# First channel product of the mixer: Strassen's seven block products in place of eight, with narrowed weights kept in DRAM for the second pair of batches

## The chip, the cores and the metric

The kernel runs on one core of one Trainium2 chip. The metric is the time of one execution on the device, in microseconds (us). Before the change it was 598.85 us in the median of three runs (597.46 to 599.61).

## What is computed

Decay attention for 4 batches, 8 heads, 768 positions and 64 dimensions, then a mixer on its output, both in float32:

```python
# attention, in 12 blocks of 64 positions, with a state kv_state carried along
out[:, :, sl] = ((qb @ kb^T) * Dmask) @ vb + (qb * lam_pow) @ kv_state
# mixer: x has 4 x 768 x 512; w_tok1 768 x 256, w_tok2 256 x 768, w_ch1 512 x 1536, w_ch2 1536 x 512
xt = x.transpose(0, 2, 1)
h = np.maximum(xt @ w_tok1, 0.0) @ w_tok2
u = x + h.transpose(0, 2, 1)
h2 = np.maximum(u @ w_ch1, 0.0) @ w_ch2
return (u + h2).astype(np.float32)
```

The mixer's weights arrive as float64. The part that the change touches is `u @ w_ch1`, 512 channels to 1536 hidden ones, for 4 x 768 positions.

## The kernel before

**Stages.** For each of 16 pairs of heads (`i` in the loop, with steps of later pairs mixed in) the kernel loads q, k and v, makes scores, state and outputs, and writes the result transposed into `uT[b]`: 128 partitions, 4 tiles of channels, 768 positions. `turn_back` turns it again into the high and low parts `xhi` and `xlo` that the token product takes. The token product (`token_hidden`, L450, and `token_out`, L470) is cut into 48 groups, which stand between the steps of the attention; the last ten of them (two hidden groups of 18 matmuls and eight output groups of 6, all of batch 3) are left for the first channel blocks. Then comes the channel part, over two thirds of the time.

**Precision.** Every product takes three matmuls in the type float32r: each operand is split in a high part (a rounded copy, by ScalarE) and a low part (the rest), and high x high, low x high and high x low are summed in PSUM. `split_block` does this for a block of `uT` (copy on ScalarE, L534; subtraction on GpSimd, L535).

**Channel part.** The 1536 hidden channels are cut into 6 groups of 256 (`NG`, with `JG` = 2 tiles of 128), the positions into 8 blocks of 384 (`blocks`: batch and half). The outer loop runs over groups, the inner over blocks. `mm1` sums 12 matmuls of 128x128 by 384 for one tile of hidden channels, ScalarE takes relu into `hh` (L649), VectorE the rest into `hl` (L650). `mm2` of the block before sums 6 matmuls for one tile of output channels, and VectorE adds them to `uT` (L671). So a group and a block have 24 matmuls of `mm1` and 24 of `mm2`.

**Weights.** For the next group `load_group` fetches four pieces of float64 words, and `narrow` turns each into float32: one step on ScalarE (L379), five on VectorE (L380, L383, L386, L389, L392), then a copy on ScalarE (L374) and a subtraction on GpSimd (L375). This is done once for a group, spread over the first blocks.

**What sets the order.** Each engine works through its instructions in the order in which the program writes them. Steps that are not tied to a matmul stand in a list `waiting` and are taken from it by `later(n)`, or are called between the products. PSUM has eight banks: four for the tag `sc`, one for `xT`, three for `sh`.

Of the kernel before, what the change touches and what calls it, by code (L numbers as in the profile page):

```python
# [21 lines left out]
def kernel(  # L22
# [23 lines left out]
    nc = tc.nc  # L46
# [74 lines left out]
    def load_kq(i):  # L121
        b, p = pairs[i]
        kn = ap.tile([P, NC, 2, D], F32, tag="kn", bufs=2, name=f"kn{i}")
        qn = ap.tile([P, S], F32, tag="qn", bufs=2, name=f"qn{i}")
# [18 lines left out]
    def load_v(i):  # L143
        b, p = pairs[i]
        vns[i] = vn = ap.tile([P, 2, NC, D], F32, tag="vn", bufs=3, name=f"vn{i}")
# [56 lines left out]
    def turn_k(i, g):  # L202
        kn, _ = loaded[i]
        if g == 0:
            kTs[i] = ap.tile([P, S], F32, tag="kT", bufs=2, name=f"kT{i}")
# [9 lines left out]
    def turn_q(i):  # L215
        qTs[i] = ap.tile([P, S], F32, tag="qT", bufs=2, name=f"qT{i}")
        if i >= NQ:
            nc.vector.transpose(out=qTs[i], in_=loaded[i][1])
        if i >= NKD:
            kTs[i] = ap.tile([P, S], F32, tag="kT", bufs=2, name=f"kT{i}")  # L220
# [61 lines left out]
    def scores(i):  # L282
        b, p = pairs[i]
        for g in range(2):
            sc = [bank("sc", f"sc{i}{g}{h}", 3 * P) for h in range(2)]
# [77 lines left out]
    def narrow(raw, a, sg, hi, lo, view):  # L363

# [3 lines left out]

        def split():
            nc.scalar.copy(out=hi, in_=view(af))  # L374
            nc.gpsimd.tensor_sub(out=lo, in0=view(af), in1=hi.bitcast(F32))  # L375

        waiting.extend(
            [
                lambda: nc.scalar.activation(af, high.bitcast(F32), AF.Abs),  # L379
                lambda: nc.vector.tensor_scalar(  # L380
                    out=sg, in0=high, scalar1=0x80000000, scalar2=None, op0=ALU.bitwise_and
                ),
                lambda: nc.vector.scalar_tensor_tensor(  # L383
                    out=sg, in0=low, scalar=29, in1=sg, op0=ALU.logical_shift_right, op1=ALU.bitwise_or
                ),
                lambda: nc.vector.tensor_scalar(  # L386
# [169 lines left out]
    for i in range(-2, NI):  # L556
# [57 lines left out]
        if 5 <= i < 9:  # L614
            load(i - 5)
# [157 lines left out]
```

## Time and profile before

| | us |
|---|---|
| median of 3 runs (lowest, highest) | 598.85 (597.46, 599.61) |
| span of the profiled execution, first to last instruction | 596.2 |
| TensorE matmul busy in it | 577.9 |
| VectorE busy | 349.7 |
| ScalarE busy | 155.2 |
| GpSimd busy | 138.7 |
| attention and most of the token product, up to the first channel matmul | 174.9 |
| from there to the end | 421.3 |

The page of the profile gives a span and no time of its own for the profiled execution; the median is 2.65 us above the span. Engines are PE (TensorE matmul), PEld (its weight loads), DVE (VectorE), ACT (ScalarE), POOL (GpSimd) and SP (the queue that issues most transfers). A row of the costliest groups has the line, engine, operation, output and inputs, shape and count, then busy time, the mean time of one, and the idle time of the engine before it with what ended it. A row of the chain of waits has a start, a duration and the work. A row of the timeline has the same with shapes. A row of a table by stretches has for each engine its busy time and, in brackets, how many instructions started. Matmul records overlap (each shows some 336 ns, and they start 173 to 176 ns apart), so the busy time of PE says little by itself.

### The profile page before, as it was taken

Reading aid. Unit: us, or ns where it says so; the run is one execution under the profiler, and the core shown is the slowest. Engines: PE = TensorE matmul, PEld = TensorE weight load, DVE = VectorE, ACT = ScalarE, POOL = GpSimd, SP = SyncE. Lnnn points to the kernel's source line nnn. Section 1 sums busy time; section 2 is a strip of 40 time slices with the busy share of each in tenths; the row PEclk is TensorE's granted clock in tenths of the full one; section 3 lists DMA queues with packets and bytes.
Section 4 is the critical chain, followed back from the end, with each engine's and each line's share of the span. In section 5 each row is a group of like instructions: output and inputs, shape, how many; then the busy total and the mean of one; then the engine's idle time right before and its main releaser. Section 6 shows DMA issues by size and latency. Waiting matters only on the chain.

```text
span 596.2 us, 10673 instructions
## 1 busy us (share of the span) xinstructions
PE 577.9 (97%) x4378; PEld 563.0 (94%) x4378; DVE 349.7 (59%) x663; ACT 155.2 (26%) x322; POOL 138.7 (23%) x131
## 2 busy tenths in 40 slices
PE   5988899999999999999999999999999999999997
PEld 4878798889999999999999999999999999999996
DVE  4797887886633666356533654356533664356664
ACT  3554434343232244112210221112210221101011
POOL 5665532462304367101100010001100010000000
PEclk9999999999999999999999999999999999999999
DMA  9998999999110111012100210012100200016667
GB/s 187 255 227 163 176 167 183 195 155 140 37 37 0 37 50 57 1 36 70 37 1 0 71 50 23 0 36 71 36 1 1 70 1 1 0 24 94 90 89 130
DMA packets 169680, 44.73 MB, mean 75 GB/s; under 512 B 162848, under 2 KB 164000, under 8 KB 169632
## 3 DMA queue, kind: packets, MB, share of 16 engines
q1 hardware_dynamic: 165488, 42.88, 37.4%
q10 hardware_dynamic: 4144, 1.18, 0.9%
q8 instruction: 34, 0.56, 0.4%
q14 instruction: 14, 0.11, 0.1%
HBM read 37.75 MB, written 6.29 MB: 74 GB/s over the span
## 4 chain that ended last, share of the span: by engine, by line
PE 88%; DMA 4%; DVE 4%; ACT 2%; issue 1%; SPq 0%; POOL 0%; DVEq 0%; ACTq 0%
PE ph L645 34%; PE po L666 34%; PE ph L450 6%; DMA kn<-in_k_dram 4%; PE pu L470 4%; PE xT L314 3%; PE sc L290 3%; PE xT L324 2%; PE xp L346 1%; PE kv L257 1%; DVE xlo L355 1%; DVE uT L389 1%; PE kt L208 1%; ACT qT L229 0%; PE qt L228 0%
## 5 line engine op out<-in xcount | busy, mean ns | idle before, releaser
L650 DVE SCALAR_TENSOR_TENSOR hl<-ph,hh 128x384 fp32r<-128x384 f32 x96 | 53.5, 558 | 164.9 <-ACT hh L649 164.9
L666 PE MATMUL po<-hh,c2h 128*128 128x384 f32 x384 | 129.4, 337 | 0.0
L645 PE MATMUL ph<-uh,c1h 128*128 128x384 f32 x384 | 129.2, 337 | 0.0
L645 PE MATMUL ph<-ul,c1h 128*128 128x384 f32 x384 | 129.2, 336 | 0.0
L645 PE MATMUL ph<-uh,c1l 128*128 128x384 f32 x384 | 129.1, 336 | 0.0
L666 PE MATMUL po<-hh,c2l 128*128 128x384 f32 x384 | 128.8, 335 | 0.0
L666 PE MATMUL po<-hl,c2h 128*128 128x384 f32 x384 | 128.6, 335 | 0.0
L649 ACT ACTIVATE hh<-ph 128x384 fp32r<-128x384 f32 x96 | 47.2, 492 | 299.6 <-PE ph L645 297.9
L671 DVE TENSOR_TENSOR uT<-po,uT 128x384 f32<-128x384 f32 x192 | 104.7, 552 | 23.5 <-PE po L666 23.4
L666 PEld LDWEIGHTS po<-hh,c2l 128*128 128x128 f32 x384 | 72.1, 188 | 0.0
L645 PEld LDWEIGHTS ph<-ul,c1h 128*128 128x128 f32 x384 | 72.1, 188 | 0.0
L666 PEld LDWEIGHTS po<-hl,c2h 128*128 128x128 f32 x384 | 72.1, 188 | 0.0
L645 PEld LDWEIGHTS ph<-uh,c1h 128*128 128x128 f32 x384 | 72.1, 188 | 0.0
L645 PEld LDWEIGHTS ph<-uh,c1l 128*128 128x128 f32 x384 | 72.1, 188 | 0.0
L666 PEld LDWEIGHTS po<-hh,c2h 128*128 128x128 f32 x384 | 72.0, 188 | 0.0
L375 POOL TENSOR_TENSOR c1l<-wa,c1h 128x512 fp32r<-128x512 f32 x10 | 12.9, 1290 | 179.9 <-ACT c1h L374 179.9
L535 POOL TENSOR_TENSOR ul<-uT,uh 128x384 fp32r<-128x384 f32 x32 | 36.0, 1154 | 37.5 <-ACT uh L534 37.5
L314 PE MATMUL xT<-a,vn 128*64 128x128 f32 x384 | 36.4, 280 | 1.9 <-ACT uT L331 1.9
L278 POOL COPY stb<-sv 64x320 f32<-64x320 f32 x32 | 26.4, 826 | 43.5 <-DVE sv L265 42.6
L299 DVE TENSOR_TENSOR a<-sc,mask 128x384 f32<-128x384 f32 x64 | 31.2, 550 | 5.7 <-PE sc L290 5.6
L324 PE MATMUL xT<-qs,stb 128*64 128x128 f32 x320 | 31.3, 273 | 0.0
L331 ACT COPY uT<-xT 128x384 f32<-128x384 f32 x32 | 15.3, 478 | 54.4 <-PE xT L324 54.4
(80 smaller groups left out, 758.1 us busy)
## 6 DMA issues: line engine op xcount, KB each, us to landing
raw<-in_moe_w_ch_dram SPq DMA_DIRECT2D x20, 512.0 KB, 3.6
vn<-in_v_dram SPq DMA_DIRECT2D x16, 384.0 KB, 5.5
kn<-in_k_dram SPq DMA_DIRECT2D x30, 192.0 KB, 5.3
out_dram<-y SPq DMA_DIRECT2D x108, 48.0 KB, 1.9
qn<-in_q_dram SPq DMA_DIRECT2D x44, 96.0 KB, 4.2
kr<-in_k_dram SPq DMA_DIRECT2D x32, 96.0 KB, 4.0
uT<-in_moe_w_ch_dram SPq DMA_DIRECT2D x4, 512.0 KB, 4.6
qn<-in_q_dram SPq DMA_DIRECT2D x8, 192.0 KB, 4.4
```

Of the source, the lines that this page charges most:

```text
L278: nc.gpsimd.tensor_copy(out=st[r, :, h, :], in_=sv[r].rearrange("p (e c) -> p c e", c=NC - 1))
L299: nc.vector.tensor_mul(out=a, in0=sc[h].rearrange("p (c i) -> p c i", i=P), in1=mask[:, 2 * p + h, None, :].broadcast_to([P, 3, P]),)
L314: nc.tensor.matmul(out=xT[h * D : (h + 1) * D, cs], lhsT=vns[i][:, h, c, :], rhs=weights_of[i, g, h][:, cg, :], start=(cg == 0), stop=False,)
L324: nc.tensor.matmul(out=xT[h * D : (h + 1) * D, cs], lhsT=st[:, c - 1, h, :], rhs=qss[i][:, c - 1, :], start=False, stop=(cg == 2),)
L450: nc.tensor.matmul(out=ph, lhsT=w[:, c, fs], rhs=x[:, c], start=(i == 0), stop=(i == 3 * NC - 1))
L470: nc.tensor.matmul(out=pu, lhsT=h[:, kk, cs], rhs=w[:, kk, ss], start=(i == 0), stop=(i == 3 * NK - 1))
L535: nc.gpsimd.tensor_sub(out=ul[:, t], in0=ub[:, t], in1=uh[:, t].bitcast(F32))
L645: nc.tensor.matmul(out=ph, lhsT=w[:, ct, js], rhs=x[:, ct], start=(i == 0), stop=(i == 11))
L649: nc.scalar.activation(hh, ph, AF.Relu)
L650: nc.vector.scalar_tensor_tensor(out=hl, in0=ph, scalar=0.0, in1=hh.bitcast(F32), op0=ALU.max, op1=ALU.subtract)
L666: nc.tensor.matmul(out=po, lhsT=w[:, jj, cs], rhs=h, start=(i == 0), stop=(i == 3 * JG - 1))
L671: nc.vector.tensor_add(out=ub, in0=po, in1=ub)
```

## The change

For each group of hidden channels the product of 2x2 blocks of channels by 2x2 blocks of (channel, position half) is made by Strassen's scheme in Winograd's form. A unit is now a group and a whole batch: seven products of 6 matmuls (`m1` to `m7`, 42 in all) take the place of eight (48). The sums around them are made on VectorE: of the weights once for a group (`split_c1`: four sums in place, so 7 block operands where there were 4), of `uT` once for a batch (`build`: four differences `t1` to `t4` and seven operands of 768 columns, each a copy on ScalarE and a subtraction on GpSimd or VectorE), and of the products in each unit (`u2`, `u3`, `c22`, `c21`, `c12`). Three of the four hidden quadrants no longer come straight from PSUM: ScalarE takes relu in place, copies, and GpSimd subtracts. The second channel product keeps its 48 matmuls for a unit, but works on pairs of banks, with one addition of 768 columns for two tiles.

The operands of two batches fill the memory, so batches 0 and 1 go through all six groups first (units 0 to 11, two for a group, the weights of the next group narrowed meanwhile, and those of four groups written to DRAM by `save`), then batches 2 and 3 (units 12 to 23) through the groups backwards, with `restore` reading them again. The operands of batch 0 are made within the last attention step, those of batch 1 between the last ten token groups, which now all stand ahead of unit 0, those of batches 2 and 3 in units 10 to 12.

```diff
+    def split(hi, lo, src):
+        nc.scalar.copy(out=hi, in_=src)
+        nc.gpsimd.tensor_sub(out=lo, in0=src, in1=hi.bitcast(F32))
...
+        return [                                     # split_c1
+            lambda: split(c1h[:, A11], c1l[:, A11], a11),
+            lambda: split(c1h[:, A12 : A22 + 1], c1l[:, A12 : A22 + 1], v[1]),
+            lambda: nc.vector.tensor_add(out=a22, in0=a21, in1=a22),
+            lambda: nc.vector.tensor_sub(out=a21, in0=a11, in1=a21),
+            lambda: nc.vector.tensor_sub(out=a11, in0=a22, in1=a11),
+            lambda: nc.vector.tensor_sub(out=a12, in0=a12, in1=a11),
+            lambda: split(c1h[:, S2 : S3 + 1], c1l[:, S2 : S3 + 1], v[0]),
+            lambda: split(c1h[:, S4 : S1 + 1], c1l[:, S4 : S1 + 1], v[1]),
+        ]
...
+        def part(o, src):                            # in build
...
+            nc.scalar.copy(out=hi, in_=src)
+            eng = nc.vector if o in on_vector else nc.gpsimd
+            eng.tensor_sub(out=lo, in0=src, in1=hi.bitcast(F32))
...
+        if i == 14:
+            waiting.extend(first[x] for x in ("t1", "t2", "T2", "T1", "t3", "T3", "t4", "T4", "B22"))
...
+    parts = build(1, 1, on_vector=("T2", "T1"))
+    order = deque(parts[x] for x in ("t1", "B11", "t2", "T2", "B21", "T1", "t3", "T3", "t4", "T4", "B22"))
+    while groups:
+        order.popleft()()
+        groups.popleft()()
...
+    def hidden_parts(n, q, src):
...
+        nc.scalar.activation(src, src, AF.Relu)
+        nc.scalar.copy(out=hh, in_=src)
+        nc.gpsimd.tensor_sub(out=hl, in0=src, in1=hh.bitcast(F32))
...
+        def m1():
+            at["a"] = bank("sh", f"pa{n}", SB)
+            prod(key, at["a"], A11, "B11", True)
+            nc.scalar.copy(out=temp("s1"), in_=at["a"])
+
+        def m6():
+            at["b"] = bank("sh", f"pb{n}", SB)
+            prod(key, at["b"], S2, "T2", True)
+            nc.vector.tensor_add(out=temp("u2"), in0=at["b"], in1=at["s1"])
+
+        def m2():
+            prod(key, at["a"], A12, "B21", False)
...
+        def m5():
+            at["c"] = bank("sh", f"pc{n}", SB)
+            prod(key, at["c"], S1, "T1", True)
+            nc.vector.tensor_add(out=temp("c22"), in0=at["c"], in1=at["u3"])
+            hidden_parts(n, "22", at["c22"])
...
+        def m3():
+            prod(key, at["c"], S4, "B22", False)
+            nc.vector.tensor_add(out=temp("c12"), in0=at["c"], in1=at["u2"])
+            hidden_parts(n, "12", at["c12"])
...
+    def save(g):
...
+            nc.sync.dma_start(out=saved[g][x], in_=src.bitcast(F32))
...
+    SLOTS = ("m1", "m6", 0, 1, "m2", "m7", 2, "m5", "m4", 3, "m3")
```

A number in `SLOTS` is a pair of output tiles of the unit before (12 matmuls); `background(n)` puts the other steps behind these slots. In units 0 to 9 the narrowing of all four pieces of the next group falls on two units, where it fell on eight blocks: the first two pieces in the even unit, the sums and the other two in the odd one.

How the instructions stand, at three places. First VectorE at the end of the attention, before the change: `hl<-ph` (L455) is a token group, `xlo` (L355) the turning back of the last pair of heads, L650 and L671 belong to the channel part.

```order
L455 SCALAR_TENSOR_TENSOR hl_2337<-ph_2371,hh_2336 128x256
L355 TENSOR_TENSOR xlo_2307<-xp_2406,xhi_2306 128x3x128
L355 TENSOR_TENSOR xlo_2307<-xp_2412,xhi_2306 128x3x128
L650 SCALAR_TENSOR_TENSOR hl_2444<-ph_2430,hh_2443 128x384
L455 SCALAR_TENSOR_TENSOR hl_2337<-ph_2455,hh_2336 128x256
```

The same place after it; `th` and `tl` hold the differences `t1` to `t4` of a batch, `T2l` and `T1l` are low parts.

```order
L451 SCALAR_TENSOR_TENSOR hl_2314<-ph_2348,hh_2313 128x256
L554 TENSOR_TENSOR th_2383<-uT_60 128x768
L554 TENSOR_TENSOR tl_2385<-uT_60,th_2383 128x768
L564 TENSOR_TENSOR T2l_2388<-tl_2385,T2h_2387 128x768
L361 TENSOR_TENSOR xlo_2284<-xp_2391,xhi_2283 128x3x128
L564 TENSOR_TENSOR T1l_2398<-th_2383,T1h_2397 128x768
L554 TENSOR_TENSOR th_2383<-uT_60 128x768
L361 TENSOR_TENSOR xlo_2284<-xp_2406,xhi_2283 128x3x128
L570 TENSOR_TENSOR tl_2385<-tl_2385,uT_60 128x768
L554 TENSOR_TENSOR th_2427<-uT_61 128x768
L451 SCALAR_TENSOR_TENSOR hl_2314<-ph_2429,hh_2313 128x256
```

Three operations of 768 columns now stand ahead of the first `xlo` and two more ahead of the second, and the next token group no longer has a channel product in front of it.

Second, ScalarE just behind that: the last copies for batch 1 (L562) and the first steps of unit 0 after the change (no such rows stood there before).

```order
L562 CAST T3h_2530<-th_2427 128x768
L562 CAST T4h_2551<-tl_2475 128x768
L562 CAST B22h_2563<-uT_61 128x768
L741 COPY s_0_2579<-pa_2572 128x384
L752 ACTIVATE h11h_2597<-pa_2572 128x384
```

The copy `s1` of unit 0, for which `m2` waits, stands behind all copies for batch 1.

Third, VectorE while weights are narrowed. Before, in a block of the second group:

```order
L650 SCALAR_TENSOR_TENSOR hl_3404<-ph_3390,hh_3403 128x384
L380 TENSOR_SCALAR ws_3310<-raw_3308 128x512
L383 SCALAR_TENSOR_TENSOR ws_3310<-raw_3308,ws_3310 128x512
L671 TENSOR_TENSOR uT_61<-po_3410,uT_61 128x384
L386 TENSOR_SCALAR wa_3309<-wa_3309 128x512
L671 TENSOR_TENSOR uT_61<-po_3419,uT_61 128x384
L389 TENSOR_SCALAR wa_3309<-wa_3309 128x512
```

After, in the first half of unit 3, an odd one (L514 to L517 are the four sums of the weights, L805 the additions to `uT`):

```order
L746 TENSOR_TENSOR u_3_3018<-pb_3011,s_3_3005 128x384
L514 TENSOR_TENSOR cs<-cs 128x2x128
L515 TENSOR_TENSOR cs<-cs 128x2x128
L516 TENSOR_TENSOR cs<-cs 128x2x128
L517 TENSOR_TENSOR cs<-cs 128x2x128
L805 TENSOR_TENSOR uT_60<-po_3024,uT_60 128x2x384
L805 TENSOR_TENSOR uT_60<-po_3042,uT_60 128x2x384
L379 TENSOR_SCALAR cs<-cs 128x512
L382 SCALAR_TENSOR_TENSOR cs<-cs 128x512
L753 SCALAR_TENSOR_TENSOR h11l_3067<-pa_2998,h11h_3066 128x384
L385 TENSOR_SCALAR cs<-cs 128x512
L759 TENSOR_TENSOR u_3_3077<-pb_3011,s_3_3005 128x384
```

Where one piece was narrowed in a block, two pieces and the sums fall into this unit, ahead of the additions that free the PSUM banks.

More of the change, by code (lines that the diff above doesn't have):

```diff
@@ L284, in scores @@
         for g in range(2):
-            sc = [bank("sc", f"sc{i}{g}{h}", 3 * P) for h in range(2)]
+            pair = two_banks(f"sc{i}{g}", 3 * P)
+            sc = [pair[:, h] for h in range(2)]
             for c in range(3):
@@ new lines @@
+    parts = build(1, 1, on_vector=("T2", "T1"))
[3 more added lines that the diff above has]
+        groups.popleft()()
+    while order:
+        order.popleft()()
+    p1.close()
+    cp = ctx.enter_context(tc.tile_pool(name="cp", bufs=1, side="right", reuse_waits="tile"))
+    cs = cp.tile([P, 2560], U32, name="cs")
+    LAST = len(blocks) - 1
+    NP1 = NG * 2
+    units = [(g, b) for g in range(NG) for b in (0, 1)] + [(g, b) for g in reversed(range(NG)) for b in (2, 3)]
@@ L634, with prod @@
+    NU = len(units)
     hs = {}
-    def mm1(g, k, jj):
-        uh, ul = uhl[k]
+    def prod(nm, to, a, o, start):
+        g, b = nm
         c1h, c1l, _, _ = weights[g]
-        js = slice(jj * P, (jj + 1) * P)
-        nm = f"{g}{k}{jj}"
-        ph = bank("sh", f"ph2{nm}", SB)
+        uh, ul = ops[b][o]
         i = 0
-        for ct in range(4):
+        for t in range(2):
             for w, x in ((c1h, uh), (c1l, uh), (c1h, ul)):
-                nc.tensor.matmul(out=ph, lhsT=w[:, ct, js], rhs=x[:, ct], start=(i == 0), stop=(i == 11))
+                nc.tensor.matmul(
+                    out=to, lhsT=w[:, a, t], rhs=x[:, t], start=(start and i == 0), stop=(i == 5),
+                    skip_group_check=not start,
+                )
@@ new lines, with run @@
+    steps = {}
+    later_parts = deque()
+    def run(n, slots):
+        ev, at, ms = background(n), 0, mixing(n)
+        for x in slots:
+            if isinstance(x, str):
+                ms[x]()
+                at += T_M
+            else:
+                out_pair(x[0], x[1])
+                at += T_P
+            while ev and ev[0][0] <= at:
+                ev.popleft()[1]()
+        while ev:
+            ev.popleft()[1]()
+    run(0, ("m1", "m6", "m2", "m7", "m5", "m4", "m3"))
+    for n in range(1, NU - 1):
+        run(n, [x if isinstance(x, str) else (n - 1, x) for x in SLOTS])
```

436 lines of the change are left out of this document (279 added, 157 removed).

## The prediction

> **What bounds the kernel now.** I read the page's busy times and chain first, then the chain of waits in order of time, then the table by stretches for the other engines, and last the groups and the timeline for durations.
>
> ```profile
> PE 577.9 (97%) x4378; PEld 563.0 (94%) x4378; DVE 349.7 (59%) x663; ACT 155.2 (26%) x322; POOL 138.7 (23%) x131
> PE ph L645 34%; PE po L666 34%; PE ph L450 6%; DMA kn<-in_k_dram 4%; PE pu L470 4%; PE xT L314 3%; PE sc L290 3%; PE xT L324 2%; PE xp L346 1%; PE kv L257 1%; DVE xlo L355 1%; DVE uT L389 1%; PE kt L208 1%; ACT qT L229 0%; PE qt L228 0%
> ...
> 254.73 2.08 PE ph L645 x12
> 256.81 2.08 PE po L666 x12
> ...
> 288.08 2.12 PE ph L645 x12
> 290.20 2.11 PE po L666 x12
> ...
> 212.60:246.10 33.50, 33.50 (x192) 33.50 (x192) 21.16 (x39) 12.57 (x27) 22.90 (x19) 1.00 0.17 48
> 317.70:584.00 266.30, 266.30 (x1526) 266.30 (x1525) 141.17 (x276) 45.23 (x88) 15.47 (x12) 1.00 0.19 38
> ```
>
> The chain is two thirds L645 and L666, each row beginning where the one before ends: in the channel part nothing but TensorE's rate counts. Twelve matmuls take 2.08 us in some stretches and 2.12 in others, 173.3 and 176.7 ns each; the stretches alternate half and half, so I use 174.8. In the last row DVE is busy 53% and POOL 6%. But in the row above, where the blocks are split and weights narrowed together, POOL is busy 68% and DVE 63%, and PE still never waits.
>
> **What is taken away.** 42 matmuls for 48, in 24 units: 144 fewer, x 174.8 ns = **-25.2 us** (-25.0 to -25.4 at the two rates). The 2160 that stay lie on operands in other places; were all fast or all slow it would be -3.2 or +4.1 us more. I take 0 and keep both ends for the range.
>
> **What is added** falls on DVE, ACT and POOL, and costs only where PE comes to wait. Durations:
>
> ```profile
> L671 DVE TENSOR_TENSOR uT<-po,uT 128x384 f32<-128x384 f32 x192 | 104.7, 552 | 23.5 <-PE po L666 23.4
> L650 DVE SCALAR_TENSOR_TENSOR hl<-ph,hh 128x384 fp32r<-128x384 f32 x96 | 53.5, 558 | 164.9 <-ACT hh L649 164.9
> L218 DVE STREAM_TRANSPOSE qT<-qn 128x768 f32<-128x768 f32 x11 | 10.5, 955 | 2.1 <-DMA qn<-in_q_dram 2.1
> L678 DVE STREAM_TRANSPOSE y<-uT 128x384 f32<-128x384 f32 x28 | 16.2, 579 | 1.1 <-DMA out_dram<-y 0.2
> L190 DVE TENSOR_TENSOR lamp<-lamp 128x256 f32<-128x256 f32 x1 | 0.4, 424 | 0.0
> L190 DVE TENSOR_TENSOR lamp<-lamp 128x128 f32<-128x128 f32 x1 | 0.3, 291 | 0.0
> L383 DVE SCALAR_TENSOR_TENSOR ws<-raw,ws 128x512 uint32<-128x512 uint32 x20 | 13.9, 693 | 0.7
> L392 DVE SCALAR_TENSOR_TENSOR wa<-wa,ws 128x512 uint32<-128x512 uint32 x20 | 13.8, 689 | 0.0
> L380 DVE TENSOR_SCALAR ws<-raw 128x512 uint32<-128x512 uint32 x20 | 8.4, 418 | 0.0
> L386 DVE TENSOR_SCALAR wa<-wa x20: 415/419/1285, 201.0 to 489.9; 128x512 f32<-128x512 f32 x20
> L534 ACT CAST uh<-uT 128x384 fp32r<-128x384 f32 x32 | 14.1, 517 | 0.0
> L374 ACT CAST c1h<-wa 128x512 fp32r<-128x512 f32 x10 | 6.2, 621 | 12.3 <-DVE wa L392 12.3
> L535 POOL TENSOR_TENSOR ul<-uT,uh x32: 997/1018/1504, 126.4 to 239.8; 128x384 fp32r<-128x384 f32 x32
> L375 POOL TENSOR_TENSOR c1l<-wa,c1h 128x512 fp32r<-128x512 f32 x10 | 12.9, 1290 | 179.9 <-ACT c1h L374 179.9
> ...
> 10.07 1.95 DVE L299 TENSOR_TENSOR a<-sc,mask 128x384 f32<-128x384 f32 x4 [3.42 <-PE sc L290]
> ```
>
> By the slopes between shapes, 768 columns take about 0.96 us on DVE (0.29 and 0.42 us for 128 and 256; L218's 0.955 agrees), 0.83 on ACT (0.52 and 0.62 for 384 and 512) and 1.8 on POOL (1.02 and 1.29). These are estimates from those rows. L299's four take 1.95 us, 0.47 a step where one takes 0.55, so rows that don't depend on each other overlap by 0.08 us.
>
> **The door between DVE and POOL.**
>
> ```profile
> 199.56 4.58 POOL L535 TENSOR_TENSOR ul<-uT,uh 128x384 fp32r<-128x384 f32 x4 [9.16 <-ACT uh L534]
> 201.02 1.28 DVE L386 TENSOR_SCALAR wa<-wa 128x512 f32<-128x512 f32 x1
> 202.69 0.54 DVE L671 TENSOR_TENSOR uT<-po,uT 128x384 f32<-128x384 f32 x1
> ...
> 212.07 0.69 DVE L383 SCALAR_TENSOR_TENSOR ws<-raw,ws 128x512 uint32<-128x512 uint32 x1
> 213.14 0.79 DVE L386 TENSOR_SCALAR wa<-wa 128x512 f32<-128x512 f32 x1
> ...
> 212.14 5.25 POOL L535 TENSOR_TENSOR ul<-uT,uh 128x384 fp32r<-128x384 f32 x4 [4.15 <-ACT uh L534]
> ```
>
> A DVE step that reads and writes SBUF alone takes 1.28 us in place of 0.42 while POOL subtracts, and POOL's four take 5.25 us in place of 4.1 (4 x 1.02) where DVE's step came first. L671, with one operand in PSUM, keeps its 0.54. So such steps take turns with POOL. From the rows, one may begin some 0.13 us before the other ends (1.28 - 0.42 = 0.86 of POOL's 1.02 is waited for).
>
> I laid the four in-order queues out with these durations, in the order that the program now has.
>
> *End of the attention.*
>
> ```profile
> 172.74 0.42 DVE L455 SCALAR_TENSOR_TENSOR hl<-ph,hh 128x256 fp32r<-128x256 f32 x1 [3.16 <-ACT hh L454]
> 174.77 1.21 DVE L355 TENSOR_TENSOR xlo<-xp,xhi 128x384 fp32r<-128x384 f32 x2 [1.61 <-ACT xhi L354]
> 174.87 2.11 PE ph L645 x12
> ```
>
> Before, both `xlo` end at 175.98 and 2.11 us of L645 cover them. Now DVE is free at 173.16 and runs `t1` to 174.1, `t2` to 175.1; ACT copies `T2h` to 176.0, DVE makes `T2l` to 177.0, the first `xlo` to 177.5, `T1l` to 178.4, `t3` to 179.4; ACT `T3h` to 180.3 and `xhi`; the second `xlo` ends at 181.3. The token group that needs them could start at 174.4 and reach its second half 1.1 us later. It waits 3.2 and then 2.7 us: **+5.9**. Then: `hl` of this group, which frees a bank, stands on ACT behind `B22h` of batch 0, which waits for two POOL subtractions of 1.8 us; with the additions of the output groups behind `T2l`, `T1l`, `t3` this makes PE wait **+4.3** among the ten groups. In unit 0, `s1` stands on ACT behind `B22h` of batch 1, which waits for POOL again, and no output pairs lie between the products: **+3.1**. In unit 1, the `hl` of quadrant 21 comes late from the same POOL queue: **+2.9**. Together +16.2. Without turns at the door the same layout gives +11.4; longer hops between engines (0.1 us in place of 0.04) give +17.6.
>
> *Units 2 to 9.* DVE in an odd unit: five additions x 0.552, one L650 0.558, four wide additions x 0.95, ten narrowing steps 2 x 2.64 (0.42 + 0.69 + 0.42 + 0.42 + 0.69), four sums x 0.42, = 13.9 us, less some 20 overlaps of 0.08: 12.3, in a unit of 90 x 0.1748 = 15.7 us. POOL: three x 1.02 and one of 256 and five of 512 columns, 0.75 + 5 x 1.29, = 10.3 us. Steps of both that take turns: 5.3 + 1.7 + 10.3 = 17.3, less 20 handovers x 0.13 = 14.7. So DVE, its waits of 0.4 to 0.9 for POOL added, is full in odd units; even units have 3 us of POOL. PE then waits in them for the bank additions: 0.3 a unit, x 8 = **+2.4** (0 to 8.4 between no turns and longer hops).
>
> *Units 10 and 11.* DVE 7.1 + 6 x 0.96 = 12.9, then 7.1 + 3 x 0.96 + 8 x 0.58 = 14.6; POOL 3 x 1.02 + 4 x 1.8 = 10.3 each, all taking turns with the differences: **+3.7** (0 to 4.8).
>
> *End.* Quadrant 12 passes relu, copy and subtraction after `m3` (0.55 + 0.5 + 0.5 + 1.0) where L649 and L650 did it in 1.05: **+0.5** after 2.1 us of cover.
>
> *Hidden.* Four saves of 2.9 MB on SP's queue, and as many restores:
>
> ```profile
> raw<-in_moe_w_ch_dram SPq DMA_DIRECT2D x20, 512.0 KB, 3.6
> GB/s 187 255 227 163 176 167 183 195 155 140 37 37 0 37 50 57 1 36 70 37 1 0 71 50 23 0 36 71 36 1 1 70 1 1 0 24 94 90 89 130
> ```
>
> At 255 GB/s a save takes 11 us; the piece issued behind it is wanted some 15 us after the save starts. 0; if that cover fails, DVE stands at its raw words for up to 2 us in four units. Restores have two units. The attention gains four sums and 768 columns on POOL, 0 to 1: PE has idle slices there, I take 0.
>
> Sum: -25.2 + 16.2 + 2.4 + 3.7 + 0.5 = **-2.4 us**, from the span of 596.2 to 593.8; the median lies 2.65 above the span: **596 us**.
>
> **A rule against the change.** The Trainium skill ("SBUF — State Buffer", Who interferes with whom) says that GpSimd and VectorE share a pair of ports as an exclusive lock, for VectorE's two-port modes and for two SBUF inputs against a GpSimd read. The trace agrees (0.42 to 1.28 us, 5.25 for four). Taken strictly, for the whole instruction, an odd unit's 17.3 us of such steps exceed its 15.7 by 1.6; by that rule five odd units would add some 8 in place of 2.4, about 602.
>
> **Rivals.** *Faster (0.27):* PE waits only at the stage's start, as without turns: -25.2 + 11.4 + 0.5 = -13.3, 585.5. For it: PE waited nowhere in 212.6 to 246.1, with both engines above 60%. Against: no addition there had seven products hanging on it. *Slower (0.25):* DVE is the pace of the odd units. It decides once handovers and waits bring an odd unit above 15.7 + the 2 us that the even one spares. With +17.6, +8.4, +4.8, +0.5: +6.1, 605. For it: 14.7 of 15.7 at the door; against: the even unit's room. *Not as said:* that fewer matmuls would not shorten PE's work; the program has 144 fewer, so under 0.02. *A lower granted clock after waits:*
>
> ```profile
> 592.00:594.00 2.00, 0.48 (x3) 0.24 (x3) 0.56 (x1) 0.00 (x0) 0.00 (x0) 0.88 0.80 248
> 594.00:596.20 2.20, 0.00 (x0) 0.00 (x0) 0.00 (x0) 0.00 (x0) 0.00 (x0) 0.50 0.33 89
> ```
>
> The column behind the engines is the granted clock: 1.00 in the channel part, 0.88 and 0.50 only once PE had stood idle for some 2 us at the very end. The layout's longest waits are 3.2 and 2.7 us, so a slice or two at half speed, some 2 us, could be added there; I leave that in the slower rival's chance.
>
> **Numbers.** The case of the sum has 0.46, with its own range of 591 to 602. 0.3% of the time, 1.8 us, is about what a measurement can tell: faster is below 597.0. Faster: half of the sum's case and nearly all of the faster rival, 0.50; same 0.18; slower 0.32. The range: the faster rival with some of the fast rate, 584, to the slower one with some of the slow rate, 608.
>
> **What would show it.** Right: 42 products a unit at 173 to 177 ns; PE's waits of 5 to 6 us at the first hidden group behind the attention, on DVE `xlo`; waits in unit 0 on `s1`; no PE wait in units 14 to 22. DVE above 85% in odd units 3 to 9, TENSOR_SCALAR rows far above 0.42. Wrong: waits on raw words from DMA, POOL rows that stay at 1.0 beside DVE, or a stage start without waits.

## The result, and the profile after

The changed kernel takes 608.11 us in the median of four runs (606.48 to 609.2), the kernel before 599.05 beside it: a ratio of 1.0153 (95% interval 1.0129 to 1.0177), 9 us slower. The forecast was 596, with a range of 584 to 608. The profiled execution has a span of 607.4 us, 11.2 over the span of before, and its own time is 609.2. That is the longest of the four, so some 2 of the 11.2 us come from which execution was profiled: the medians are 9.06 apart.

The chain of the page before by engine, then the page after, busy times and chain:

```profile
PE 88%; DMA 4%; DVE 4%; ACT 2%; issue 1%; SPq 0%; POOL 0%; DVEq 0%; ACTq 0%
```

```profile
PE 568.9 (94%) x4234; PEld 543.3 (89%) x4234; DVE 414.5 (68%) x663; ACT 215.6 (36%) x426; POOL 238.0 (39%) x205
PE 54%; DVE 26%; issue 5%; ACT 5%; POOL 4%; DMA 4%; SPq 1%; POOLq 0%; DVEq 0%; ACTq 0%
```

The 144 matmuls are gone (4378 to 4234), but PE holds less of the chain: it fell from 88% to 54%, and VectorE rose from 4% to 26%. The table by stretches shows where. First two stretches of before (a step of the attention between two sets of scores, and as many matmuls as the second row below has, counted from the last scores), then the same two after, followed by units 0 and 1, units 2 to 9, 10 and 11, and 12 to 22. The columns are PE, weight loads, VectorE, ScalarE, GpSimd, then the granted clock.

```profile
103.33:115.03 11.70, 11.45 (x132) 10.29 (x131) 9.70 (x20) 5.24 (x11) 4.38 (x4) 1.00 1.11 187
157.61:187.40 29.79, 29.69 (x284) 28.34 (x284) 11.21 (x22) 9.86 (x23) 6.41 (x7) 1.00 0.07 21
```

```profile
105.92:122.05 16.13, 12.65 (x131) 10.66 (x130) 12.98 (x24) 5.81 (x12) 7.02 (x7) 0.96 0.89 176
165.04:203.90 38.86, 33.59 (x284) 30.36 (x283) 25.33 (x36) 12.88 (x22) 12.81 (x8) 0.91 0.05 15
203.90:231.73 27.83, 24.20 (x134) 22.92 (x133) 21.26 (x37) 11.98 (x23) 14.98 (x12) 1.00 0.44 161
231.73:363.26 131.53, 129.62 (x722) 125.36 (x721) 107.00 (x177) 53.55 (x105) 55.59 (x49) 1.00 0.38 130
363.26:398.81 35.55, 32.98 (x181) 31.21 (x181) 32.05 (x41) 16.62 (x29) 25.75 (x16) 1.00 0.18 26
398.81:572.34 173.53, 173.53 (x992) 173.53 (x991) 85.28 (x122) 47.52 (x94) 42.72 (x39) 1.00 0.28 80
```

The last row is the change as it was meant: 11 units in 173.53 us, 15.78 each with 90 matmuls (175.3 ns a matmul), no idle time, VectorE at 49%. A unit of 96 took 16.78 before (96 x 0.1748). All that is lost lies ahead of it, and at the end. Set against the terms of the prediction (a unit without waits is 15.78, a part of it by its matmuls):

| part | forecast, us | measured, us | working of the measured |
|---|---|---|---|
| matmuls taken away | -25.2 | -24.1 | 24 x (96 x 0.1748 - 90 x 0.1753) |
| attention, to the last scores | 0 | +7.4 | 165.04 - 157.61 |
| from there to unit 0 | +10.2 | +9.1 | 38.86 - 29.79 |
| unit 0 | +3.1 | +1.5 | 8.82 - 42 x 0.1753 |
| unit 1 | +2.9 | +3.2 | 19.01 - 15.78 |
| units 2 to 9 | +2.4 | +5.3 | 131.53 - 8 x 15.78 |
| units 10 and 11 | +3.7 | +4.0 | 35.55 - 2 x 15.78 |
| end | +0.5 | +4.7 | 3.1 behind the last transposes, 1.6 of waits ahead of them |
| sum | -2.4 | +11.1 | the spans differ by 11.2 |

One profile is one execution. In the profiles of the kernels below, stretches that an edit leaves as they are spread too: unit 1 from 19.0 to 21.6 us, units 2 to 9 from 129.8 to 131.5, the end behind the last transposes from 7.0 to 7.9. From the last scores to unit 0 they agree (38.8 to 38.9).

### The profile page after: what moved, and what is told of

Same layout as the page of the kernel before. It is cut to its first block, busy times and chain, and to the rows that moved or that the text cites. A ratio compares the mean times of both kernels' runs of the same rounds, so it can differ in the third digit from the quotient of the medians.

```text
span 607.4 us, 10680 instructions
## 1 busy us (share of the span) xinstructions
PE 568.9 (94%) x4234; PEld 543.3 (89%) x4234; DVE 414.5 (68%) x663; ACT 215.6 (36%) x426; POOL 238.0 (39%) x205
## 4 chain that ended last, share of the span: by engine, by line
PE 54%; DVE 26%; issue 5%; ACT 5%; POOL 4%; DMA 4%; SPq 1%; POOLq 0%; DVEq 0%; ACTq 0%
PE po L790 19%; PE ph L446 6%; PE pa L713 5%; PE pc L713 4%; PE pb L713 4%; DVE uT L805 4%; PE pu L466 3%; PE sc L296 3%; PE xT L320 3%; DVE cs L379 3%; PE pd L713 2%; DMA cs<-in_moe_w_ch_dram 2%; POOL c1l L371 2%; DVE cs L382 2%; PE xT L330 2%
## 5 line engine op out<-in xcount | busy, mean ns | idle before, releaser
L805 DVE TENSOR_TENSOR uT<-po,uT 128x768 f32<-128x768 f32 x94 | 89.1, 952 | 60.3 <-PE po L790 60.1
L726 POOL TENSOR_TENSOR h22l<-c,h22h 128x384 fp32r<-128x384 f32 x24 | 26.3, 1097 | 152.7 <-ACT h22h L725 152.7
L724 ACT ACTIVATE c<-c 128x384 f32<-128x384 f32 x72 | 37.8, 525 | 104.4 <-DVE c L764 65.5
L726 POOL TENSOR_TENSOR h12l<-c,h12h 128x384 fp32r<-128x384 f32 x24 | 24.4, 1017 | 30.7 <-PE pa L713 18.7
L752 ACT ACTIVATE h11h<-pa 128x384 fp32r<-128x384 f32 x24 | 11.7, 487 | 65.4 <-PE pa L713 65.4
L446 PE MATMUL ph<-xhi,w1h 128*128 128x256 f32 x96 | 30.2, 315 | 3.8 <-ACT xhi L360 3.2
L726 POOL TENSOR_TENSOR h21l<-c,h21h 128x384 fp32r<-128x384 f32 x24 | 26.4, 1101 | 17.0 <-ACT h21h L725 11.6
L446 PE MATMUL ph<-xlo,w1h 128*128 128x256 f32 x96 | 28.9, 302 | 0.6 <-DVE xlo L361 0.6
L446 PE MATMUL ph<-xhi,w1l 128*128 128x256 f32 x96 | 28.7, 299 | 0.0
L296 PE MATMUL sc<-qT,kT 64*128 64x128 f32 x384 | 28.0, 297 | 0.2 <-ACT qT L234 0.2
L296 PEld LDWEIGHTS sc<-qT,kT 64*128 64x128 f32 x384 | 24.9, 203 | 3.5 <-issue 2.0
```

The source lines that it names most:

```text
L296: nc.tensor.matmul(out=sc[h][:, c * P : (c + 1) * P], lhsT=kTs[i][r, cs], rhs=qTs[i][r, cs], start=True, stop=True,)
L446: nc.tensor.matmul(out=ph, lhsT=w[:, c, fs], rhs=x[:, c], start=(i == 0), stop=(i == 3 * NC - 1))
L724: nc.scalar.activation(src, src, AF.Relu)
L726: nc.gpsimd.tensor_sub(out=hl, in0=src, in1=hh.bitcast(F32))
L805: nc.vector.tensor_add(out=ub, in0=po, in1=ub)
```

## The experiments

Each is the changed kernel with one edit, unless it says otherwise; a time is the median of its runs, and the figures behind it are its ratio to the kernel before and the 95% interval of that. Stretches are from the profiled execution of each. Three kernels leave something out of the computation, as their expectations say; they measure a cost and are no versions to use.

### The attention: +7.4 us where 0 was forecast

Timeline rows of the changed kernel in the step that grew from 11.70 to 16.13 us (start, duration, work; in brackets the idle time before it and what ended it):

```profile
108.54 1.76 DVE L514 TENSOR_TENSOR uT<-uT 128x256 f32<-128x256 f32 x1 [0.64 <-POOL c1l L371]
111.13 1.94 DVE L305 TENSOR_TENSOR a<-sc,mask 128x384 f32<-128x384 f32 x4
115.87 0.62 ACT L370 CAST c1h<-uT 128x512 fp32r<-128x512 f32 x1 [2.23 <-DVE uT L517]
117.57 0.46 ACT L360 CAST xhi<-xp 128x384 fp32r<-128x384 f32 x1
118.07 0.56 DVE L361 TENSOR_TENSOR xlo<-xp,xhi 128x384 fp32r<-128x384 f32 x1 [1.90 <-ACT xhi L360]
```

The sums of group 0's weights (L514 to L517) stand in this step. The copy that needs the last sum waits for 2.23 us on ScalarE, and `xhi`, whose transposes end at 113.6, stands behind it; on VectorE the first sum takes 1.76 us in place of 0.42, beside GpSimd's `qs`. The first experiment undoes the order on ScalarE alone.

```diff
-            waiting.extend(split_c1(weights[0], a0, a1))
+            s = split_c1(weights[0], a0, a1)
+            a2 = w[:, 512:1024]
+            p = narrow_piece(raw[1], a2, sg)
+            waiting.extend(s[:6] + p[:2] + s[6:7] + p[2:4] + s[7:] + p[4:])
...
-            waiting.extend(narrow_piece(raw[1], a0, sg))
```

> Group 0's weight sums in the attention, in another order: the steps of the third piece are put between the four sums and the two copies that need them, and that piece is narrowed into its own memory, so that it no longer waits for the splits. The same instructions on every engine. Theory (ScalarE's queue: the copy xhi stood behind a copy that waited for the last sum, and behind a step that waited for GpSimd): the stretch between two scores that grew from 11.70 to 16.13 us falls to 12.5 or less, the kernel to 603 to 604.5. Rival (the sums and subtractions themselves are too much for VectorE, GpSimd and the door there): the stretch stays above 14.5, the kernel above 606.

The step came to 15.29 us, the kernel to 605.61 (1.0121 of before, 1.0078 to 1.0165). `xhi` now came at 113.8, but PE waited for `hl` and the additions on VectorE: my theory of ScalarE's order fell. The rival's number for the step stood, and the kernel came just under its 606. In the ten other kernels that leave this step as it is, it took 15.6 to 16.5 us, so the new order gave little if anything. So the sums, and the splits that need them, were moved to a time at which VectorE has room; the third and fourth piece are narrowed into memory of their own.

```diff
         if i == 7:
-            waiting.extend(narrow_piece(raw[1], a1, sg))
+            waiting.extend(narrow_piece(raw[1], a1, s0))
...
-            waiting.extend(split_c1(weights[0], a0, a1))
...
         if i == 11:
+            later(99)
+            waiting.extend(split_c1(weights[0], a0, a1))
+        if i == 13:
             later(99)
```

> The narrowed pieces of group 0 are kept apart in the scratch memory, and its four sums and four splits are issued two attention steps later, where VectorE is 64% busy in place of 80 to 87%; the same instructions otherwise. Theory (the sums, two of them held at the door, made VectorE the late engine of that step; the order on ScalarE alone gave only 0.8 of 4.4 us): the stretch between two scores falls from 16.13 to 11.7 to 12.2 us, no later one grows by over 0.5, the kernel comes to 602.5 to 604.5. Rival (they cost as much wherever they stand): another stretch grows by over 2 us, the kernel stays above 606.

The step came to 11.68 us and no other grew; PE's only wait in it was 0.2 us. The kernel: 602.87 (1.0076, 1.0055 to 1.0098), 5.2 us less. The same stretch in it:

```profile
105.00:117.00 12.00, 11.75 (x134) 10.47 (x134) 9.45 (x18) 4.51 (x10) 1.69 (x3) 1.00 1.04 210
```

The four small sums and their splits, at a step where VectorE has little to spare, cost 4.4 us (3.9 to 4.8 by the other kernels); two steps later they cost nothing. Memory of its own for the third piece is not the reason, since the first experiment had that too. The other 3 us of this part are not the change's alone: 1.5 are the granted clock (below), and the ten steps ahead took 94.9 to 97.5 us over the profiles of all the kernels here, with nearly the same instructions.

### From the last scores to unit 0: +9.1 us

The chain of waits after, from the last transposes to the first whole token group:

```profile
180.60 0.88 DVE th L554
181.50 0.97 DVE tl L554
182.49 0.84 ACT T2h L562
183.35 0.96 DVE T2l L564
184.31 0.47 DVE xlo L361
184.78 0.88 DVE T1l L564
185.68 0.97 DVE th L554
186.67 0.83 ACT T3h L562
187.50 0.39 ACT xhi L360
187.93 5.54 PE ph L446 x27
```

Rows of 0.02 us of "issue" between them are left out. This is the layout of the prediction row by row: `t1`, `t2`, `T2h`, `T2l`, first `xlo`, `T1l`, `t3`, `T3h`, `xhi`. Whether the order or the amount of work decides was tried by putting batch 0's builds behind both turnings-back.

```diff
-        if i == 14:
+        if i == NI - 1:
             waiting.extend(first[x] for x in ("t1", "t2", "T2", "T1", "t3", "T3", "t4", "T4", "B22"))
```

> The differences and operands of batch 0 stand behind both turnings-back of the last pair of heads, no longer ahead of xlo; all else as in the changed kernel. From the last transposes (181.1 us) to the first product of unit 2 (231.7) it took 50.6 us where 36.9 us of matmuls are. Theory (VectorE, GpSimd and the door have more to do there than PE, in any order): the waits on xhi and xlo go, those on hl of the token group and on unit 0 grow by as much, the stretch stays within 2 us, the kernel at 606 to 610. Rival (only the order costs): the stretch loses 5 to 6 us, the kernel comes to 602 to 603.

The stretch to unit 2 became 67.8 us (66.7 in the changed kernel), the kernel 609.54 (1.018, 1.016 to 1.0199). The waits moved from `xhi` (3.2 us) to `hl` (5.8 us in one wait), as expected of an amount of work, not of an order. The next one keeps PE's clock up.

```diff
+    def warm(n):
+        idle = two_banks(f"idle{n}", SB)
+        for m in range(n):
+            nc.tensor.matmul(out=idle[:, 0], lhsT=w2h[:, 0, :P], rhs=w2h[:, 0, :SB], start=True, stop=True)
...
+    warm(6)          # ahead of the ten groups; warm(10) in the middle of the first
```

> 16 matmuls with no use, 384 columns each, stand in front of the first of the last ten token groups and in its middle, where PE waits 1.4 and 1.8 us for xhi; all other work as in the changed kernel. Theory (PE's waits lower its granted clock: 21 matmuls of that stretch took 214 ns in place of 119): they come back to 119 ns, the stretch from the last scores to unit 0 falls from 38.86 to 36.5 to 37.3 us, the kernel by 1.5 to 2.2. Rival (what these waits let slip is waited for anyway a little later, by hl on VectorE): the stretch stays above 38.3.

Rows by stretches of the slow part of the changed kernel, which holds 23 of the 36 matmuls of the two hidden groups, and of all 36 in this one, with ten of the idle ones between them. In the changed kernel the 36 stand from 183.75 to 193.30 us.

```profile
185.50:192.30 6.80, 5.02 (x23) 4.63 (x22) 4.39 (x6) 3.15 (x6) 2.85 (x2) 0.50 0.02 4
```

```profile
182.41:190.27 7.86, 6.93 (x46) 6.20 (x47) 6.08 (x7) 3.13 (x5) 2.16 (x2) 1.00 0.01 3
```

The clock stayed at 1.00 and the token groups were done 1.7 us earlier, counted from the last scores; then PE waited twice for VectorE's additions, 1.3 and 1.2 us where it had been once 1.2, the clock fell there instead, and the stretch to unit 0 took 39.70 us. Kernel: 607.74 (1.0158, 1.0135 to 1.0182). So the lower clock is real, but here it filled time in which PE would have waited. Two kernels then took work away, from VectorE and from GpSimd.

```diff
-            "T1": lambda: part("T1", t["h"]),        # and T2, T3, T4 likewise; t1 to t4 not computed
+            "T1": lambda: part("T1", t["h"] if b > 1 else b12),
```

> The eight differences of batches 0 and 1 are left out of the computation: T1 to T4 are copied and split from the blocks of uT themselves. VectorE loses 8 steps of 768 columns, 0.96 us each; ScalarE and GpSimd keep all of theirs. The stretch from the last scores to the first product of unit 2 took 66.7 to 69.2 us so far, 13 to 15 more than its matmuls. Theory (VectorE's queue is the bound of that stretch): it comes to 60 to 63.5 us, the kernel to 601 to 604. Rival (GpSimd's low parts, 1.8 us each, one behind the other, are the bound): 65 or more, the kernel above 605.5.

```diff
+            if b < 2 and o not in on_vector:
+                nc.scalar.copy(out=lo, in_=src)
+                return
             eng.tensor_sub(out=lo, in0=src, in1=hi.bitcast(F32))
```

> For batches 0 and 1 the ten low parts that GpSimd made are a second copy by ScalarE (0.84 us in place of 1.8), so they hold the high part's value and the low part is left out of the computation; VectorE keeps its twelve steps, and no longer meets GpSimd at the door. Theory (VectorE's queue is the bound, the door adds to it): the stretch from the last scores to unit 2, 66.7 to 69.2 us, comes to 63.5 to 66.5, the kernel to 604 to 606.5. Rival (GpSimd is the bound): 62 or less, the kernel below 602.5.

From the last scores to unit 0, without the differences, and without GpSimd's low parts:

```profile
162.41:195.30 32.89, 31.00 (x283) 28.36 (x283) 18.20 (x29) 13.95 (x24) 15.05 (x9) 1.00 0.06 17
```

```profile
162.53:201.08 38.55, 33.14 (x284) 30.23 (x283) 22.45 (x36) 17.19 (x28) 1.54 (x2) 0.91 0.05 15
```

Without the differences the stretch to unit 0 lost 6.0 us and to unit 2 came to 60.9; the kernel to 599.46 (1.0008, 0.9995 to 1.0021), below the 601 of the theory: 2.6 us of its span were won in the attention, which the edit doesn't touch. With GpSimd almost idle (1.54 us) it lost 0.3, and to unit 2 it took 68.0, where 63.5 to 66.5 were expected; 607.69 (1.0152, 1.0124 to 1.0181): ScalarE, with the copies, now let PE wait 4.2 us for `xhi` in place of 3.2. Neither the theory's number nor the rival's came; 1.1 of the 68.0 us are unit 1, which ran at a lower clock here (0.92 for 1.00). So VectorE's queue is a bound here, and the copies on ScalarE alternate with it. That GpSimd's work costs nothing is not shown, because ScalarE got it. What the turns at the door cost (4.8 us in my layout, with units 0 and 1) was not measured by itself: this kernel took them away and put ScalarE's copies in their place.

### Units 1 to 9

```diff
+    def twice(hi, lo, src):
+        nc.scalar.copy(out=hi, in_=src)
+        nc.scalar.copy(out=lo, in_=src)
...
-                c1 = split_c1(weights[to], a0, a1)
+                c1 = split_c1(weights[to], a0, a1, twice)    # in odd units; split_c2 likewise
```

> In the odd units 1 to 9 the low parts of the narrowed weights are a second copy by ScalarE in place of GpSimd's subtraction (so they hold the high part's value: the low part is left out of the computation). GpSimd loses 0.75 + 5 x 1.29 us a unit, ScalarE gains 3. Theory (GpSimd, through the door and by coming late with the low parts of the hidden quadrants, makes PE wait): units 2 to 9, which take 131.5 us where 125.9 of matmuls are, come to 126.5 to 127.5 and unit 1 loses 1 us, the kernel is at 602 to 604. Rival (VectorE's own work fills the odd units): they stay above 130, the kernel at 606 or more.

The rows are units 3 and 4 of the changed kernel and as many matmuls of this one:

```profile
248.20:281.30 33.10, 32.49 (x183) 31.30 (x182) 26.83 (x45) 13.45 (x27) 13.95 (x13) 1.00 0.43 145
```

```profile
256.00:287.50 31.50, 31.50 (x182) 31.50 (x181) 25.71 (x48) 16.09 (x32) 6.50 (x6) 1.00 0.45 162
```

Units 2 to 9 took 126.25 us: every wait was gone. VectorE is 82% busy in the second row and PE never waits. The kernel: 600.23 (1.0033, 1.002 to 1.0047), below the 602 of the theory; units 10 and 11 lost 1.9 us too, 33.61 for 35.55. How GpSimd does it is seen in an odd unit of the changed kernel:

```profile
252.46 1.99 POOL L371 TENSOR_TENSOR c1l<-cs,c1h 128x256 fp32r<-128x256 f32 x2
254.49 0.42 DVE L514 TENSOR_TENSOR cs<-cs 128x256 f32<-128x256 f32 x1 [2.11 <-POOL c1l L371]
256.21 1.81 DVE L805 TENSOR_TENSOR uT<-po,uT 128x768 f32<-128x768 f32 x2
257.94 1.45 DVE L379 TENSOR_SCALAR cs<-cs 128x512 uint32<-128x512 uint32 x1
```

The first sum overwrites a piece that GpSimd still reads and waits 2.11 us; both additions that free PSUM's banks (L805) stand behind four sums. Then L379 takes 1.45 us in place of 0.42, beside GpSimd. The order was changed:

```diff
-                add(12, c1[2], c1[3], c1[4], c1[5])
-                add(24, pb[0] if False else c1[6], c1[7])
+                add(36, c1[2], c1[3], c1[4], c1[5])
+                add(42, c1[6], c1[7])                # the later steps one or two slots later too
```

> In the odd units 1 to 9 the four sums of the weights stand behind the additions of the first two output pairs on VectorE, in place of ahead of them, and what follows moves by one or two slots. In unit 1 the sums waited 1.6 us for GpSimd, and PE 2.7 us for the additions behind them. Theory (it is this order in VectorE's queue): units 0 and 1, which took 27.8 to 30.4 us together, come to 25 to 26.5, units 2 to 9 (131.5) to at most 130.5, the kernel to 604 to 606. Rival (the raw words come late to unit 1, so all behind them is late in any order): units 0 and 1 stay above 27.5.

Units 0 and 1 came to 25.83 us, and the odd units 3 to 9 to 15.7 to 15.8, without a wait. But the even ones grew to 17 (there `s1` now waited on ScalarE behind a copy of the weights), so that units 2 to 9 stayed at 131.07, half a microsecond over the bound of the theory; 606.31 (1.0124, 1.0097 to 1.015). What GpSimd's load does was tried from two more sides: by taking the quadrants from it, and by giving VectorE the weights.

```diff
-        nc.gpsimd.tensor_sub(out=hl, in0=src, in1=hh.bitcast(F32))
+        eng = nc.vector if n < 10 and n % 2 else nc.gpsimd
+        eng.tensor_sub(out=hl, in0=src, in1=hh.bitcast(F32))
```

> In the odd units 1 to 9 the low parts of three hidden quadrants are subtracted by VectorE in place of GpSimd; the low parts of the weights stay on GpSimd. GpSimd loses 3 x 1.02 us of such a unit, VectorE gains 3 x 0.55. Theory a (the quadrants queue behind the weights on GpSimd): units 2 to 9, 131.5 us with 125.9 of matmuls, come to 126.5 to 128.5. Theory b (VectorE and ScalarE wait for the weights' low parts, at the door and for the splits): they stay at 130 to 133.

```diff
+    def split_v(hi, lo, src):
+        nc.scalar.copy(out=hi, in_=src)
+        nc.vector.tensor_sub(out=lo, in0=src, in1=hi.bitcast(F32))
...
-                c1 = split_c1(weights[to], a0, a1)
+                c1 = split_c1(weights[to], a0, a1, split_v)    # in odd units; split_c2 likewise
```

> In the odd units 1 to 9 the low parts of the weights are subtracted by VectorE in place of GpSimd: 5.5 x 0.69 = 3.8 us more there, 12.3 + 3.8 = 16.1 in units of 15.76, and half of the unit's steps no longer meet GpSimd at the door. If VectorE's own time counts, the odd units come to 16.5 to 17.5 and units 2 to 9 to 131 to 135. If what counts is only the lateness of GpSimd and the door, they come to 126.5 to 128.5 as with the copies on ScalarE, the kernel to 603 to 605.

Units 2 to 9 took 138.5 us with the quadrants on VectorE (kernel 619.07; 1.0347, 1.0326 to 1.0368), more than either theory said, and 133.6 with the weights on it (609.77; 1.0191, 1.0166 to 1.0217), as expected if VectorE's own time counts. So VectorE has no time for either load. Whether the quadrants in GpSimd's queue also held PE is not shown, since VectorE's new load hides it. What is shown is that the weights' low parts on GpSimd cost these 5.3 us. They can do it by the wait for the splits and by the turns at the door; the share of the two was not separated.

### The end

Here SyncE's issues tell it. Before, 108 output transfers were issued from 531.62 us on, and the last transposes came at 591.96:

```profile
531.62 58.82 SPq L684 DMA_DIRECT2D out_dram<-y  x108
```

After, batches 2 and 3 are finished only in the last two units, and the transposes come at 600.06. SyncE issues one transfer in 0.55 us, and had 29 of them left at 588.31 us; the last, of `ylast`, stood behind them.

```profile
578.34 25.82 SPq L818 DMA_DIRECT2D out_dram<-y  x46
588.31 15.85 SPq L818 DMA_DIRECT2D out_dram<-y  x29
604.26 0.42 SPq L840 DMA_DIRECT2D out_dram<-ylast  x1
```

```diff
-            (nc.sync if t == 2 else nc.scalar).dma_start(out=to[:, :, es], in_=ylast[:, :, es])
+            nc.scalar.dma_start(out=to[:, :, es], in_=ylast[:, :, es])
```

> The third of the last output transfers is issued by ScalarE's queue in place of SyncE's, where it waited for 14 others until 604.3 us. Theory: the end then follows the last issue on ScalarE's queue as before the change (3.1 us after 601.2), so the span loses 2.5 to 3.2 us, the kernel is at 605 to 605.6. Rival (the 14 transfers themselves end no earlier, they are the end): less than 0.8 us.

The rival was right: from the last transposes to the end took 8.1 us, not less (607.05; 1.0146, 1.012 to 1.0172). The queue of the others ended as late. So half of those of the last unit but one were moved.

```diff
-                eng = nc.scalar if k == LAST - 1 and tt == 3 and m >= 2 else nc.sync
+                eng = nc.scalar if m >= 2 and (n == NU - 2 or (k == LAST - 1 and tt == 3)) else nc.sync
```

> Half of the output transfers of the last unit but one are issued by ScalarE's queue in place of SyncE's, which issues one in 0.57 us and had 28 left at 588.8 us; nothing else is changed. Theory (SyncE's rate of issue is the end; moving only the last transfer to ScalarE did not help, since the 22 others still ended at 602.4): the queue is empty by 599.5, the time from the last transposes to the end falls from 7.3 to about 4.2 us, the kernel comes to 604.5 to 605.5. Rival (the transfers share the memory's rate, or ScalarE's queue, now with 18, is late itself): under 1 us.

```profile
587.98 12.24 SPq L818 DMA_DIRECT2D out_dram<-y  x22
600.82 0.39 SPq L840 DMA_DIRECT2D out_dram<-ylast  x1
```

From the last transposes to the end it took 4.8 us in place of 7.3 (4.2 before the change), so the rate of issue was the end. The time itself, 607.19 (1.0146, 1.0114 to 1.0178), hardly shows it. Ahead of the transposes 0.55 us were lost, since ScalarE's relu of the last quadrant now stands behind four issues, and in the profiled execution unit 1 took 21.57 us in place of 19.01, at a granted clock of 0.84.

### Put together, and half of the change

The first has the sums of group 0 later, the sums of the other weights behind the additions, and the last transfers on two queues.

> Seven products in all units, with the three moves of instructions together: group 0's sums two attention steps later, the sums of the weights behind the additions of two output pairs, half of the last transfers on ScalarE's queue. Same work as in the changed kernel. If the three costs are independent they add: 607.4 less 5.5, 2.0 and 2.3 us, a span of 597 to 598.5, a time of 598 to 600, no faster than before the change, and slower than with eight products for batches 0 and 1 (592.5). If one takes another's place: above 601.

A span of 598.7 and a time of 599.61 (1.0018, 1.0003 to 1.0033): 8.7 us of span less, of 9.8 expected from the three. The attention gave 6.5 of it, units 0 and 1 gave 1.9. The end gave only 0.9: behind the last transposes 3.1 were won, but unit 23 ahead of them took 29.92 us in place of 27.72, at a granted clock of 0.94. With the same work as the changed kernel, seven products for all units are as fast as eight, within some 0.3%. From the last scores to unit 0 it still takes 38.84 us.

The second gives up seven products where their operands can't be made in time.

```diff
+    def quarter(n, r, c, to):                    # 12 matmuls, A21 from a tile of its own
+        rows = ((A11, "B11"), (A12, "B21")) if r == 1 else ((None, "B11"), (A22, "B21"))
...
+    PLAIN = ("q11", "q21", 0, 1, "e11", "e21", "q12", "q22", 2, 3, "e12", "e22")
+        run(n, [x if isinstance(x, str) else (n - 1, x) for x in (SLOTS if n >= NP1 else PLAIN)])
```

> Batches 0 and 1 go through their six groups with eight products, their hidden quadrants straight from PSUM as before the change; only batches 2 and 3 (units 12 to 23) use seven. No differences for batches 0 and 1, no sums of group 0 in the attention (its pieces go to memory and are summed in unit 21), two quarters of unit 0 between the token groups. Theory (the loss lies in making the operands of batches 0 and 1 at the end of the attention, and in GpSimd's load in units 1 to 11): 12 units x 6 x 0.1748 = 12.6 us of matmuls are gained, the end loses 3, units 10 to 12 up to 4: 590 to 593, faster than both. Rival (the eight-product units also wait, on VectorE's narrowing or on quadrants in one memory): above 597.

595.63 us (0.9958, 0.9945 to 0.997): faster than both, but above the expected 593. Unit 1 had a wait of 2.8 us for additions behind the sums, and ran at half clock for 3 us after it; it took 21.33 us, some 4.5 more than its 96 matmuls. The same two moves as above, with a split (of A12, A22 and A21) also moved, from 6 to 24 matmuls into the unit:

```diff
-                add(6, c1[1], c1[2])
-                add(12, c1[3], c1[4], c1[5], c1[6])
+                add(24, c1[1], c1[2])
+                add(49, c1[3], c1[4], c1[5], c1[6])     # behind the additions of two pairs; the later steps too
-                eng = nc.scalar if k == LAST - 1 and tt == 3 and m >= 2 else nc.sync
+                eng = nc.scalar if m >= 2 and (n == NU - 2 or (k == LAST - 1 and tt == 3)) else nc.sync
```

> As the kernel with eight products for batches 0 and 1, with three things moved: the sums of the weights behind the additions of the first two output pairs, A12 and A22 split 18 matmuls later, and half of the last transfers on ScalarE's queue. The version before took 595.6 us; PE waited 4.9 us in its unit 1 for additions that stood behind the sums, and 7.1 us passed between the last transposes and the end where 4.2 did before the change. Theory: both go, 588 to 591. Rival (the wait in unit 1 comes from late raw words, and the last transfers share the memory's rate): 594 or more.

592.51 us (0.9893, 0.9875 to 0.9911) beside 599.16 for the kernel before, 1.5 above the theory's bound. This is the fastest version: 1.1% less than before. Its page, and its row from about the start of unit 2 to unit 12:

```profile
PE 569.8 (97%) x4306; PEld 553.5 (94%) x4306; DVE 389.6 (66%) x627; ACT 189.0 (32%) x379; POOL 198.7 (34%) x174
PE 82%; DVE 8%; DMA 4%; ACT 2%; issue 1%; SPq 1%; ACTq 0%; POOL 0%; POOLq 0%; DVEq 0%
...
213.00:383.81 170.81, 169.26 (x967) 168.94 (x966) 135.37 (x200) 53.54 (x101) 55.54 (x41) 1.00 0.32 107
```

72 matmuls fewer than before, PE again 82% of the chain. PE idles 1.55 us in the row, in one wait of unit 2 for L862, and in units 10 and 11 not at all: the operands of batches 2 and 3 are made beside eight-product units at no cost.

## Why the prediction was wrong, step by step

- **Matmuls taken away**: right. -24.1 for -25.2; the operands in their new places gave 175.3 ns a matmul, well inside the two ends.
- **The attention at 0**: this step failed. The prediction said that PE has idle slices there, took four sums and 768 columns on GpSimd as 0 to 1, and put 0 into the sum. It did not ask what VectorE had left in that step: 9.70 of 11.70 us were taken. The stretch grew by 7.4 us. Moving the sums and their splits gave back the 4.4 us of the step, and these alone turn the sign (-2.4 + 4.4 = +2.0). Of the other 3.0, 1.5 is the granted clock.
- **From the last scores to unit 0, units 0 and 1**: forecast 16.2, measured 13.8; the layout named the waits in their order, and the experiments show a cause, work for VectorE that the other order did not hide. That the size fits is in part luck: ahead of unit 0 PE's four waits add up to 5.0 us for 10.2, and 21 matmuls at 214 ns in place of 119 add 2.0, a term that the sum did not have. In unit 1 the cause was another: not the low part of quadrant 21 but the sums ahead of the additions; behind them, units 0 and 1 took 25.83 us for 27.83. The faster rival (PE waits only at the stage's start) did not come.
- **Units 2 to 9**: PE waited for the additions, as forecast, but for more: 5.3 for 2.4, inside 0 to 8.4 (3.5 to 5.3 over the profiles of nine kernels that have the same units). The layout had the sums wait for nothing but their turn; they waited 2.11 us for GpSimd's splits, and two additions stood behind. So VectorE was 77% busy in an odd unit (12.87 of 16.76 us), not above 85% as said: it was late, not full. How much of it the turns at the door are stays open. Two figures of the layout are slips that change little: its terms add up to 14.1 us of VectorE in an odd unit, not 13.9, and 0.86 waited of 1.02 leaves a handover of 0.16, not 0.13.
- **Units 10 and 11**: 4.0 for 3.7, in part by luck: without GpSimd's work on the weights in the odd units up to 9 it was 2.1 (33.61 us), so about half comes over from unit 9. The turns with the differences were not tested by themselves.
- **The end**: this term failed too, 4.7 for 0.5. The prediction counted ScalarE and GpSimd for the last quadrant (1.6 measured) and never SyncE's queue, though the page of before shows its issues; the output of the last units falls together now. Sharing the issues took 2.5 of the 3.1 us away.
- **The slower rival** (605, VectorE the pace of the odd units) had the right side and engine, but its price was in the units, where the largest errors were not. By the rule of the Trainium skill ("SBUF — State Buffer", Who interferes with whom) taken strictly, units 2 to 9 would have lost some 8 by the prediction's estimate; they lost 5.3, between the two readings.
- **The lower clock after waits** was left inside the slower rival's chance; it came at three places ahead of unit 0, and in the one place where it was undone it was worth nothing by itself. Over a whole execution the clock was 0.98 in all four runs of the changed kernel, and 0.995 to 1.00 in those of the kernel before beside the experiments.
- **From span to time**: the 2.65 us between span and median come from two executions. Wherever both are on record for the same execution, they lie some 1.8 us apart.

## What to carry to other kernels

Fewer matmuls pay only where the engines that feed them have time in the same stretch: ask of each step that is moved what its own queue has left there (here 2.0 of 11.7 us), not whether PE has a free slice. In an in-order queue, put an operation that waits for a slower engine behind those that free the banks, and when outputs are gathered at the end, count the issues of the queue that writes them. Where the operands of the cheaper scheme can't be made in time, use it only for the part of the work behind which they can.

## What the hardware showed that was not expected

The granted clock falls to half after waits that are not long, and not every time. One wait, 2.20 us for VectorE in the attention, with the same instructions in both kernels, was followed by 18 matmuls in 3.74 us after and 2.22 before:

```profile
65.98:69.72 3.74, 3.74 (x22) 3.74 (x21) 1.40 (x3) 1.51 (x3) 3.60 (x4) 0.54 0.80 139
```

```profile
65.51:67.73 2.22, 2.22 (x21) 2.22 (x20) 1.40 (x3) 1.51 (x3) 2.08 (x3) 1.00 0.98 137
```

Of the fifteen other kernels here ten had it at that place and five had not, which alone makes 1.2 to 1.5 us between two executions. In unit 1 the same wait of 2.6 to 2.7 us stands in ten kernels: three ran the unit at a clock of 1.00 (19.0 us), six at 0.91 or 0.92 (20.1 to 20.3) and one at 0.84. The rows are unit 1 of the changed kernel, and of the one with half of the last transfers on ScalarE's queue:

```profile
212.72:231.73 19.01, 16.35 (x92) 15.71 (x91) 15.90 (x26) 7.70 (x16) 9.49 (x9) 1.00 0.61 233
```

```profile
212.40:233.97 21.57, 18.89 (x91) 18.57 (x91) 18.20 (x29) 9.22 (x18) 10.89 (x10) 0.84 0.55 210
```

The Trainium skill ("TensorE: Matmul & The Clock Gate", Part 1) says that the gate looks at free-running windows of some 3.4 us, so that the moment of a change varies between runs; that it varies agrees with these rows. It also puts the fall after at least one idle window; here waits of 2.2 and 2.7 us were enough, and the measurement decides.
